# The last expert of a mixture-of-experts stage multiplied in plain fp32, its weights loaded straight into their tiles

## The chip, the cores and the metric

The kernel runs on 1 core of one Trainium2 chip. The metric is the device time of one execution in microseconds (us); lower is better. TensorE is called PE, VectorE DVE, ScalarE ACT, GpSimd POOL, and SyncE, which issues nearly all DMAs here, SP.

## The reference

Three stages follow one another: clustered attention, a mixture of experts in which every token goes to one of 8 experts, and a dense feed-forward layer.

```python
# attention: q, k, v are (2, 8, 768, 64); a query sees only the keys of its own cluster (16 clusters)
scores = np.where(q_assign[..., :, None] == k_assign[..., None, :], q @ k.T / 8, -1e9)
x = softmax(scores) @ v                     # tokens: (1536, 512)
# experts: 8 experts, w1[e] is (512, 1024), w2[e] is (1024, 512)
e_idx = np.argmax(x @ w_gate, axis=1)
for e in range(8):
    h = np.maximum(x[mask] @ w1[e], 0.0)
    out[mask] = gate_w[mask, None] * eom[mask, e, None] * (h @ w2[e])
# dense layer: w_in is (512, 2048), w_out is (2048, 512), both given as float64
h = out @ w_in
y = (h * sigmoid(1.702 * h)) @ w_out
```

## The kernel before, in words

The attention takes the first 280 us or so and the change does not touch it. The experts follow, sorted by the number of their tokens: the expert in place 0 has room for 304 tokens, the next ones for 256, 224, 208, 192, 176 and 160, and the last, in place 7 (called E7 here; E6 is the one in front of it), for 128. The work is written for a manual schedule, so each engine does its instructions in the order of the code (with the interleaving of the tile framework at a few places).

**A product.** The experts and the dense layer work with high and low parts: a number is split into a rounded part (type fp32r) and the rest, and a product is high times high, high times low and low times high. `product` does this for an expert with at most 256 tokens in two matmuls: the high weights times the low and the high part of the tokens side by side (2n columns, L1162), and the low weights times the high part of the tokens (n columns, L1163). The two halves of the sum are added afterwards by `total`: ACT copies one half out of PSUM (L1168), DVE adds it to the other (L1169).

**A step.** An expert has four chunks of 256 hidden columns, each with two halves of weights of 512 KB: half 0 from `w1`, half 1 from `w2`. The loop over `g` takes eight steps for an expert, one for each 128 hidden columns; E7 has g = 56 to 63. In step g, `win_h` does four products (w1, accumulated into a bank `ph`), `total` and the Relu (L1183) by ACT and DVE, and later `rest` (L1186, DVE) makes the low part of the hidden values. `finish` does the four products of w2 (`win_y`, into four banks `py`) for step g - 2. In the second step of an expert (`turned`) `finish` goes first; so `py` of E6 ends in step 57, and `win_out` empties its four banks by `total`, and then E7's first `win_y`, in step 58, can write them.

**Weights.** `loads_to` lets SP load halves into four buffers `raw` in the order of a list; `split_pair` makes the high part by ACT (L1064, a cast of 128x1024) and the low part by POOL, or by DVE in every fourth step (L1067). The tiles of split weights come from the pool `wp`, three buffers for each half, `w0` and `w1`, each `[128, 2, 1024]`: one chunk's high and low part. The split for step g + 3 of the list is written at the head of step g, ahead of the step's own work on ACT:

```python
split_low = split_pair(ekeys[n_], half, None, nc.vector if g % 4 == 3 else nc.gpsimd, g % 4 == 3)
loads_to(g + 7)
```

The tokens of the next expert are turned by PE and split by ACT (L1150) and DVE (L1151) in `win_x`; for E7 this lies in step 54. `dense_step` spreads the conversion of the dense layer's float64 weights over the steps (`wide_stages`: L125 to L135, then L1099 by ACT and L1100 by POOL).

**The dense layer.** 48 steps of 24 matmuls with 512 columns (L1347 to L1349 and L1445 to L1447). The first of them, `dense_in(0)`, stands between E7's last two groups of `win_y`.

Of the kernel before, what the change touches and what calls it, by code (L numbers as in the profile page):

```python
# [46 lines left out]
def attention_moe_ffn(ctx: ExitStack, tc: tile.TileContext, q, k, v, centroids, w_gate, w_og, w1, w2, w_in, w_out, out):  # L47
# [981 lines left out]
    def bank(name):  # L1029
        pool, tag = banks[0]  # L1030
        banks.rotate(-1)
        return pool.tile([128, 512], F32, name=name, tag=tag)
# [74 lines left out]
    def wb(key, part, i):  # L1107
        return pairs[key]["w", 1][:, part].rearrange("p (i d) -> p i d", i=2)[:, i]


    def win_load(ex_row, n, one_tile=False, pieces=False):
        nr = -(-n // 128)
        if one_tile:
            x = hp.tile([128, 2 * CAP], F32R, name="ht", tag="ht")[:, None, :DM].bitcast(F32)
        else:
            x = xrp.tile([128, WR, DM], F32, name="xr", tag="xr")
        d = {"n": n, "nr": nr, "x": x, "rows": [128] * (nr - 1) + [n - 128 * (nr - 1)]}

        def rows_of(r0, m, p, names):
            row = nc.s_assert_within(ex_row + r0 * 128, 0, E * NT - 128, skip_runtime_bounds_check_because="inside the rows of an expert") if r0 else ex_row  # L1120
            x = nc.sync.dma_start(out=d["x"][:p, r0:r0 + m], in_=xd[bass.ds(row + FIRST, m * p)].rearrange("(r p) c -> p r c", p=p)).ins
            for nm in scatters[len(names):]:
                tc.declare_no_dep(x, nm, reason="an expert with 128 rows in these groups: later tokens have other rows")
            need(x, names)

        if pieces:

            p = (n - 128) // (nr - 1)
            d["rows"] = [128] + [p] * (nr - 1)
            assert sum(d["rows"]) == n and LEAST >= 128  # L1130
            rows_of(0, 1, 128, scatters[:-GROUPS[-1][2]])
            d["rest"] = lambda: rows_of(1, nr - 1, p, scatters)
        else:
            rows_of(0, nr, 128, scatters)
        return d

    def win_x(d, r):
        if r == 0:

            side = CAPS.index(d["n"]) % 2 if d["n"] in CAPS else 0  # L1140
            d["t"] = xp.tile([128, 8 * CAPS[side]], F32R, name="t", tag=f"t{side}", bufs=1)[:, :8 * d["n"]].rearrange("p (k n) -> p k n", k=4)
        m, r0 = d["rows"][r], sum(d["rows"][:r])
        xs = d["x"][:m, r]
        pt = bank("pxt")
        for k in range(4):
            nc.tensor.transpose(pt[:, k * 128:k * 128 + m], xs[:, k * 128:(k + 1) * 128], ident[:m, :m])
        n = d["n"]
        hi = d["t"][:, :, n + r0:n + r0 + m]
        src = pt.rearrange("p (k n) -> p k n", k=4)[:, :, :m]
        nc.scalar.copy(hi, src)  # L1150
        nc.vector.tensor_tensor(d["t"][:, :, r0:r0 + m], src, f32(hi), op=ALU.subtract)  # L1151

    def product(ps, n, w_hi, w_lo, t, first, last):


        lo, hi = t[:, 0:n], t[:, n:2 * n]
        if n > 256:
            nc.tensor.matmul(ps[:, :n], w_hi, hi, start=first, stop=False)
            nc.tensor.matmul(ps[:, :n], w_hi, lo, start=False, stop=False)
            nc.tensor.matmul(ps[:, :n], w_lo, hi, start=False, stop=last)  # L1160
        else:
            nc.tensor.matmul(ps[:, :2 * n], w_hi, t, start=first, stop=False)  # L1162
            nc.tensor.matmul(ps[:, n:2 * n], w_lo, hi, start=False, stop=last)  # L1163
# [8 lines left out]
    def win_h(d, key, i, defer=False):  # L1172
        n = d["n"]
        ph = bank("ph")
        for k in range(4):
            product(ph, n, wa(key, 0, k, i), wa(key, 1, k, i), d["t"][:, k], k == 0, k == 3)
        ht = hp.tile([128, 2 * CAP], F32R, name="ht", tag="ht")[:, :2 * n]
        lo, hi = ht[:, 0:n], ht[:, n:]
        t = ph[:, :n]
        if n <= 256:  # L1180

            total(ph, n, t)
        nc.scalar.activation(hi, t, AF.Relu)  # L1183

        def rest():
            nc.vector.scalar_tensor_tensor(lo, t, 0.0, f32(hi), op0=ALU.max, op1=ALU.subtract)  # L1186
        if defer:
            return ht, rest
        rest()
        return ht  # L1190

    def win_y(d, key, i, ht, first, last):
        if first:
            d["py"] = sums()
        for m in range(4):
            ms = slice(m * 128, (m + 1) * 128)
            product(d["py"][m], d["n"], wb(key, 0, i)[:, ms], wb(key, 1, i)[:, ms], ht, first, last)

    def win_out(d, col, defer=False, eng=None):
        n = d["n"]  # L1200
        cs = bass.ds(col, n)
        if n > 256:
            ys = [py[:, :n] for py in d["py"]]
        else:
            room = xp.tile([128, 4 * max(CAPS[1:])], F32, name="room", tag="room", bufs=1)[:, :4 * n].rearrange("p (m n) -> p m n", m=4)
            ys = [total(d["py"][m], n, room[:, m]) for m in range(4)]

        def rest():
            if n <= 256:
                nc.scalar.copy(yth[:, :, cs], room)  # L1210
                (eng or nc.gpsimd).tensor_tensor(ytl[:, :, cs], room, f32(yth)[:, :, cs], op=ALU.subtract)
                return
            for m, y in enumerate(ys):
                nc.scalar.copy(yth[:, m, cs], y)
                nc.vector.tensor_tensor(ytl[:, m, cs], y, f32(yth)[:, m, cs], op=ALU.subtract)
        if defer and n <= 256:
            return rest
        rest()

    cx = ExitStack()  # L1220
    raw = cx.enter_context(tc.tile_pool(name="raw", reuse_waits="tile", bufs=4))
    ekeys = [("e", e, c) for e in range(E) for c in range(4)]
# [1 line left out]


    order = [(0, 0), (1, 0), (0, 1)]
    for n in range(2, len(ekeys) + 1):
        order += [(n, 0)] * (n < len(ekeys)) + [(n - 1, 1)]

    def loads_to(n):  # L1230

        while loaded[0] < min(n, len(order)):
            n_, half = order[loaded[0]]
            load_half(ekeys[n_], half, exps[ekeys[n_][1]], rawd if loaded[0] < 2 else None)
            loaded[0] += 1

    xp = cx.enter_context(tc.tile_pool(name="xp", reuse_waits="tile", bufs=2))
    hp = cx.enter_context(tc.tile_pool(name="hp", reuse_waits="tile", bufs=3))
    xrp = cx.enter_context(tc.tile_pool(name="xrp", reuse_waits="tile", bufs=1))
# [1 line left out]
    wins = {}  # L1241

    def win_start(e, pieces=False):
        wins[e] = win_load(nc.s_assert_within(exps[e] * NT, 0, (E - 1) * NT, skip_runtime_bounds_check_because="a row of experts"), CAPS[e], False, pieces)


    loads_to(2)
# [104 lines left out]
    with tc.manual_schedule():  # L1352
# [14 lines left out]
        for g in range(G + 2):  # L1367
# [40 lines left out]
            for f in (low, split_low, *late):  # L1408
                if f:
                    f()  # L1410
            dense_step(min(5 * e + max(0, c - 2), 40) + 3 * min(max(0, g - 61), 2))
            if g < G:
                if c == 0 and e and e + 1 < E:
                    win_start(e + 1)
                if g == 2:
                    offs = nc.values_load_multi_w_load_instructions(plan[:, E:], engines=[ACT_E, DVE_E, POOL_E], min_val=0, max_val=NT)[1]
# [111 lines left out]
```

## Time and profile before

| | before |
|---|---|
| time, median of 3 runs | 724.02 us (720.78 to 724.78) |
| time of the profiled execution | 724.04 us |
| its span, first to last instruction | 722.3 us |
| PE, busy share of the span | 97% |
| DVE, ACT, POOL | 63%, 54%, 37% |

The time of the profiled execution is 1.7 us more than its span; this much lies around the span and no view shows it. The busy shares are means over the attention, the experts and the dense layer. A matmul's end is modelled and overlaps the start of the next one, so the pace of PE is read from the starts of its instructions.

### The profile page before, as it was taken

Reading aid. Unit: us, or ns where it says so; the run is one execution under the profiler, and the core shown is the slowest. Engines: PE = TensorE matmul, PEld = TensorE weight load, DVE = VectorE, ACT = ScalarE, POOL = GpSimd, SP = SyncE. Lnnn points to the kernel's source line nnn. Section 1 sums busy time; section 2 is a strip of 40 time slices with the busy share of each in tenths; the row PEclk is TensorE's granted clock in tenths of the full one; section 3 lists DMA queues with packets and bytes.
Section 4 is the critical chain, followed back from the end, with each engine's and each line's share of the span. In section 5 each row is a group of like instructions: output and inputs, shape, how many; then the busy total and the mean of one; then the engine's idle time right before and its main releaser. Section 6 shows DMA issues by size and latency. Waiting matters only on the chain.

```text
span 722.3 us, 12542 instructions
## 1 busy us (share of the span) xinstructions
PE 699.4 (97%) x4522; PEld 577.7 (80%) x4522; DVE 452.2 (63%) x888; ACT 393.0 (54%) x789; POOL 266.4 (37%) x219
## 2 busy tenths in 40 slices
PE   8999999999999998999999998999999999999996
PEld 6777776776766777999999898888888888888885
DVE  6969788899988972344544545788564666242322
ACT  7767676666766643566777676544434353222220
POOL 2230321303280033766979889222532112020202
PEclk8999999999999998999999999999999999999999
DMA  6768869546066538566677775233634220010101
GB/s 198 170 189 273 215 225 282 153 146 181 27 171 213 196 126 269 172 229 206 199 241 232 263 235 188 89 110 68 85 59 59 60 87 30 1 59 1 59 0 59
DMA packets 70573, 105.18 MB, mean 146 GB/s; under 512 B 9627, under 2 KB 48283, under 8 KB 70507
## 3 DMA queue, kind: packets, MB, share of 16 engines
q1 hardware_dynamic: 67563, 95.94, 45.7%
q0 software_dynamic: 2944, 8.40, 3.1%
q8 instruction: 37, 0.61, 0.3%
q14 instruction: 29, 0.24, 0.1%
HBM read 70.46 MB, written 14.69 MB: 118 GB/s over the span
## 4 chain that ended last, share of the span: by engine, by line
PE 54%; issue 17%; POOL 7%; DMA 7%; DVE 6%; ACT 6%; SPq 1%; POOLq 0%; ACTq 0%; DVEq 0%
PE po L567 6%; PE pt L532 5%; PE ph L1347 4%; PE ph L1349 4%; PE ph L1348 4%; PE py L1447 3%; PE py L1445 3%; PE py L1446 3%; PE sp L515 3%; PE sp L516 3%; POOL w L1067 3%; PE py L1162 3%; PE ph L1162 2%; ACT w L1064 2%; DMA raw<-in_moe_w_dram 2%
## 5 line engine op out<-in xcount | busy, mean ns | idle before, releaser
L1067 POOL TENSOR_TENSOR w<-raw,w 128x1024 fp32r<-128x1024 f32 x51 | 128.1, 2529 | 38.3 <-ACT w L1064 25.4
L518 DVE TENSOR_REDUCE nm<-sp 128x1 f32<-128x768 f32 x96 | 91.6, 955 | 15.6 <-PE sp L516 14.4
L1430 DVE TENSOR_TENSOR sg<-ph,sg 128x512 f32<-128x512 f32 x48 | 33.2, 691 | 99.7 <-ACT sg L1429 97.5
L524 ACT ACTIVATE P<-sp,nm 128x768 f32<-128x768 f32 x96 | 87.2, 909 | 10.6 <-DVE nm L518 10.1
L532 PEld LDWEIGHTS pt<-ident,P 128*128 128x128 f32 x576 | 65.2, 141 | 27.3 <-issue 16.9
L532 PE MATMUL pt<-ident,P 128*128 128x128 f32 x576 | 82.9, 277 | 3.4 <-DVE pT L539 1.6
L1429 ACT ACTIVATE sg<-ph 128x512 f32<-128x512 f32 x48 | 28.7, 597 | 104.8 <-PE ph L1349 100.4
L1447 PE MATMUL py<-w,gl 128*128 128x512 f32 (+1 forms) x194 | 75.2, 387 | 0.0
L1445 PE MATMUL py<-w,gh 128*128 128x512 f32 (+1 forms) x194 | 75.0, 387 | 0.0
L1446 PE MATMUL py<-w,gh 128*128 128x512 f32 (+1 forms) x194 | 75.0, 387 | 0.0
L1100 POOL TENSOR_TENSOR w<-csq,w 128x512 fp32r<-128x512 f32 x24 | 32.7, 1363 | 114.5 <-ACT w L1099 114.5
L1347 PE MATMUL ph<-yth,w 128*128 128x512 f32 x192 | 74.8, 390 | 0.0
L1349 PE MATMUL ph<-yth,w 128*128 128x512 f32 x192 | 74.7, 389 | 0.0
L1348 PE MATMUL ph<-ytl,w 128*128 128x512 f32 x192 | 74.7, 389 | 0.0
L515 PE MATMUL sp<-X,Q 128*128 128x384 f32 x192 | 73.6, 384 | 0.5 <-ACT P L524 0.4
L1162 PE MATMUL py<-ht,w 128*128 128x512 f32 (+6 forms) x224 | 69.8, 367 | 3.5 <-DVE room L1169 2.0
L1064 ACT CAST w<-raw 128x1024 fp32r<-128x1024 f32 x68 | 70.5, 1042 | 4.8 <-issue 2.5
L1162 PE MATMUL ph<-t,w 128*128 128x512 f32 (+6 forms) x224 | 68.9, 366 | 1.2 <-DVE ht L1186 0.7
L567 PE MATMUL po<-pT,ld_v 128*32 128x384 f32 x768 | 68.6, 490 | 0.0
L516 PE MATMUL sp<-Z,Q 80*128 80x384 f32 x192 | 65.3, 340 | 1.9 <-DMA Q<-ohT 1.9
L537 ACT COPY pT<-pt 128x384 f32<-128x384 f32 x96 | 45.9, 478 | 32.7 <-PE pt L532 32.7
L539 DVE COPY pT<-pt 128x384 f32<-128x384 f32 x96 | 52.8, 550 | 8.1 <-PE pt L532 7.7
(294 smaller groups left out, 1468.7 us busy)
## 6 DMA issues: line engine op xcount, KB each, us to landing
raw<-in_moe_w_dram SPq DMA_DIRECT2D x64, 512.0 KB
raw<-in_moe_w_in_dram SPq DMA_DIRECT2D x16, 512.0 KB
raw<-in_moe_w_out_dram SPq DMA_DIRECT2D x16, 512.0 KB
xd<-zrow SPq DMA_DIRECT2D x8, 768.0 KB
Q<-Hq SPq DMA_DIRECT2D x28, 192.0 KB
ew<-in_moe_w_dram SPq DMA_DIRECT2D x9, 384.0 KB
ld_q<-in_q_dram SPq DMA_DIRECT2D x8, 384.0 KB
ld_k<-in_k_dram SPq DMA_DIRECT2D x8, 384.0 KB
```

Of the source, the lines that this page charges most:

```text
L515: nc.tensor.matmul(sp[:, n, :384], d["Q1"][:, h, cs], d["X"][:, h, ks], start=True, stop=False)
L518: nc.vector.tensor_reduce(nm, sp[:, :, :384], op=ALU.max, axis=AX.XY, negate=True)
L532: nc.tensor.transpose(pt[:, r * 128:(r + 1) * 128], L["P"][:, n, r * 128:(r + 1) * 128], ident)
L567: nc.tensor.matmul(po[32 * g:32 * g + 32, :384], v_[:, hh, tile_t(kt), 32 * a:32 * a + 32], pts[n][:, kt, :], start=kt < (2 if alone else ...
L1067: (eng or nc.gpsimd).tensor_tensor(lo, r, f32(hi), op=ALU.subtract)
L1162: nc.tensor.matmul(ps[:, :2 * n], w_hi, t, start=first, stop=False)
L1347: nc.tensor.matmul(ph, wa(key, 0, k, i), yth[:, k, cs], start=(k == 0), stop=False)
L1348: nc.tensor.matmul(ph, wa(key, 0, k, i), ytl[:, k, cs], start=False, stop=False)
L1349: nc.tensor.matmul(ph, wa(key, 1, k, i), yth[:, k, cs], start=False, stop=(k == 3))
L1445: nc.tensor.matmul(po[m][:, cs], gh[:, ms], wb(key, 0, i)[:, cs], start=first, stop=False)
L1446: nc.tensor.matmul(po[m][:, cs], gh[:, ms], wb(key, 1, i)[:, cs], start=False, stop=False)
L1447: nc.tensor.matmul(po[m][:, cs], gl[:, ms], wb(key, 0, i)[:, cs], start=False, stop=last)
```

## The change

E7 (`PLAN`) is marked `plain`. It has no high and low parts: `win_x` makes one fp32 copy of its tokens, `win_h` and `win_y` do one fp32 matmul for each product, the Relu goes straight from PSUM to the hidden values, and `win_out` takes the four banks as they are. The list of loads and splits ends with E6. In place of E7's eight halves by way of `raw`, `load_plain` lets SP load them into the same tiles of `wp`, two chunks to a tile (two DMAs of 512 KB each), after the work of steps 52, 54 and 56. The products, their number and the order of the steps stay.

```diff
--- before.py
+++ after.py
@@ -1147,6 +1147,9 @@
         n = d["n"]
         hi = d["t"][:, :, n + r0:n + r0 + m]
         src = pt.rearrange("p (k n) -> p k n", k=4)[:, :, :m]
+        if d.get("plain"):
+            nc.scalar.copy(f32(d["t"])[:, :, 0:n], src)
+            return
         nc.scalar.copy(hi, src)
         nc.vector.tensor_tensor(d["t"][:, :, r0:r0 + m], src, f32(hi), op=ALU.subtract)
 
@@ -1172,6 +1175,12 @@
     def win_h(d, key, i, defer=False):
         n = d["n"]
         ph = bank("ph")
+        if d.get("plain"):
+            ht = f32(hp.tile([128, 2 * CAP], F32R, name="ht", tag="ht"))[:, :n]
+            for k in range(4):
+                nc.tensor.matmul(ph[:, :n], wa(key, 0, k, i), f32(d["t"])[:, k, 0:n], start=k == 0, stop=k == 3)
+            nc.scalar.activation(ht, ph[:, :n], AF.Relu)
+            return ht, None
         for k in range(4):
             product(ph, n, wa(key, 0, k, i), wa(key, 1, k, i), d["t"][:, k], k == 0, k == 3)
         ht = hp.tile([128, 2 * CAP], F32R, name="ht", tag="ht")[:, :2 * n]
@@ -1194,19 +1203,22 @@
             d["py"] = sums()
         for m in range(4):
             ms = slice(m * 128, (m + 1) * 128)
+            if d.get("plain"):
+                nc.tensor.matmul(d["py"][m][:, :d["n"]], wb(key, 0, i)[:, ms], ht, start=first, stop=last)
+                continue
             product(d["py"][m], d["n"], wb(key, 0, i)[:, ms], wb(key, 1, i)[:, ms], ht, first, last)
 
     def win_out(d, col, defer=False, eng=None):
         n = d["n"]
         cs = bass.ds(col, n)
-        if n > 256:
+        if n > 256 or d.get("plain"):
             ys = [py[:, :n] for py in d["py"]]
         else:
             room = xp.tile([128, 4 * max(CAPS[1:])], F32, name="room", tag="room", bufs=1)[:, :4 * n].rearrange("p (m n) -> p m n", m=4)
             ys = [total(d["py"][m], n, room[:, m]) for m in range(4)]
 
         def rest():
-            if n <= 256:
+            if n <= 256 and not d.get("plain"):
                 nc.scalar.copy(yth[:, :, cs], room)
                 (eng or nc.gpsimd).tensor_tensor(ytl[:, :, cs], room, f32(yth)[:, :, cs], op=ALU.subtract)
                 return
@@ -1217,6 +1229,7 @@
             return rest
         rest()
 
+    PLAIN = E - 1
     cx = ExitStack()
     raw = cx.enter_context(tc.tile_pool(name="raw", reuse_waits="tile", bufs=4))
     ekeys = [("e", e, c) for e in range(E) for c in range(4)]
@@ -1224,8 +1237,8 @@
 
 
     order = [(0, 0), (1, 0), (0, 1)]
-    for n in range(2, len(ekeys) + 1):
-        order += [(n, 0)] * (n < len(ekeys)) + [(n - 1, 1)]
+    for n in range(2, 4 * PLAIN + 1):
+        order += [(n, 0)] * (n < 4 * PLAIN) + [(n - 1, 1)]
 
     def loads_to(n):
 
@@ -1234,6 +1247,17 @@
             load_half(ekeys[n_], half, exps[ekeys[n_][1]], rawd if loaded[0] < 2 else None)
             loaded[0] += 1
 
+    def load_plain(half, c0):
+
+        w = f32(wp.tile([128, 2, 1024], F32R, name=f"w{half}", tag=f"w{half}"))
+        ex = exps[PLAIN]
+        for n in range(2):
+            src = pair_of(w1[bass.ds(ex, 1)].rearrange("o d f -> (o d) f"), w2[bass.ds(ex, 1)].rearrange("o f d -> (o f) d"), c0 + n)[half]
+            nc.sync.dma_start(out=w[:, n].rearrange("p (g n) -> p g n", g=src.shape[1]), in_=src)
+            pairs.setdefault(("e", PLAIN, c0 + n), {})["w", half] = w[:, n:n + 1]
+
+    plain_at = {52: [(0, 0)], 54: [(0, 2), (1, 0)], 56: [(1, 2)]}
+
     xp = cx.enter_context(tc.tile_pool(name="xp", reuse_waits="tile", bufs=2))
     hp = cx.enter_context(tc.tile_pool(name="hp", reuse_waits="tile", bufs=3))
     xrp = cx.enter_context(tc.tile_pool(name="xrp", reuse_waits="tile", bufs=1))
@@ -1241,7 +1265,9 @@
     wins = {}
 
     def win_start(e, pieces=False):
+        assert e != PLAIN or CAPS[e] <= 128
         wins[e] = win_load(nc.s_assert_within(exps[e] * NT, 0, (E - 1) * NT, skip_runtime_bounds_check_because="a row of experts"), CAPS[e], False, pieces)
+        wins[e]["plain"] = e == PLAIN
 
 
     loads_to(2)
@@ -1409,6 +1435,8 @@
                 if f:
                     f()
             dense_step(min(5 * e + max(0, c - 2), 40) + 3 * min(max(0, g - 61), 2))
+            for x in plain_at.get(g, ()):
+                load_plain(*x)
             if g < G:
                 if c == 0 and e and e + 1 < E:
                     win_start(e + 1)
```

What this moves is seen on three engines. In the rows, `w` with a number is a tile of weights; the diff above shifts line numbers, so L1168, L1169 and L1183 of before read L1171, L1172 and L1192 after, L1162 and L1163 read L1165 and L1166, and E7's own Relu is L1182. The words in brackets are what an instruction waits for: engines, or DMA queues (DMAHW).

ACT, from step 54 to the first emptying of E6's banks (`hs<-py`) in step 57, before:

```order
L1064 CAST w_6228<-raw 128x1024 [waits DMAHW3_49,Pool_49]
L1150 CAST t<-pxt 128x4x128 [waits PE_49]
L1168 COPY hs<-ph 128x160 [waits PE_49,Activation_49]
L1183 ACTIVATE ht<-ph 128x160 [waits DVE_49]
L1064 CAST w_6264<-raw 128x1024 [waits DMAHW4_49,Pool_49]
L1168 COPY hs<-ph 128x160 [waits PE_49,Activation_49]
L1183 ACTIVATE ht<-ph 128x160 [waits DVE_49]
L1064 CAST w_6294<-raw 128x1024 [waits DMAHW5_49,Pool_49]
L1168 COPY hs<-ph 128x128 [waits PE_49,Activation_49]
L1183 ACTIVATE ht<-ph 128x128 [waits DVE_49]
L1064 CAST w_6322<-raw 128x1024 [waits DMAHW6_49]
L1168 COPY hs<-py_6128 128x160 [waits PE_49,Activation_49]
```

The same place in the changed kernel:

```order
L1151 COPY t<-pxt 128x4x128 [waits PE_49]
L1171 COPY hs<-ph 128x160 [waits PE_49,Activation_49]
L1192 ACTIVATE ht<-ph 128x160 [waits DVE_49]
L1171 COPY hs<-ph 128x160 [waits PE_49,Activation_49]
L1192 ACTIVATE ht<-ph 128x160 [waits DVE_49]
L1182 ACTIVATE ht<-ph 128x128 [waits PE_49,Activation_49]
L1171 COPY hs<-py_6126 128x160 [waits PE_49,Activation_49]
```

The four casts of weights between these rows are gone, E7's first Relu waits for PE and no longer for a sum by DVE, and it needs no `hs` ahead of it.

PE at the beginning of E7 (step 56: `win_h` of E7, then the first product of `win_y` for E6's step 54), before:

```order
L1162 MATMUL ph<-t,w_6169 128x256 [waits DVE_49]
L1163 MATMUL ph<-t,w_6169 128x128 [waits Pool_49]
L1162 MATMUL ph<-t,w_6169 128x256
L1163 MATMUL ph<-t,w_6169 128x128
...
L1162 MATMUL py_6128<-ht,w_6199 128x320 [waits DVE_49]
L1163 MATMUL py_6128<-ht,w_6199 128x160 [waits Pool_49]
```

And after:

```order
L1181 MATMUL ph<-t,w_6193 128x128 [waits DMAHW2_49,Activation_49]
L1181 MATMUL ph<-t,w_6193 128x128 x3
L1165 MATMUL py_6126<-ht,w_6165 128x320 [waits DVE_49]
L1166 MATMUL py_6126<-ht,w_6165 128x160 [waits Pool_49]
```

Eight matmuls have become four of 128 columns; they wait for a DMA and for ACT where they waited for DVE and POOL.

SP, E7's loads up to the first load of the dense layer that has to be converted (L111), before:

```order
L1050 DMA raw<-in_moe_w_dram 128x2x512 [waits DMAHW7_49,DVE_49,Activation_49]
L1050 ISA
L1050 DMA raw<-in_moe_w_dram 128x4x256 [waits DMAHW1_49,Pool_49]
L1050 ISA
L1050 DMA raw<-in_moe_w_dram 128x2x512 [waits DMAHW2_49,Pool_49]
L1050 ISA
L1050 DMA raw<-in_moe_w_dram 128x4x256 [waits DMAHW3_49,Pool_49]
L111 DMA raw<-in_moe_w_in_dram 128x2x512 [waits DMAHW0_49]
```

And after (`w_6250` holds half 0 of E7's chunks 2 and 3, `w_6253` half 1 of chunks 0 and 1; ahead of them stand the two loads of `w_6193`, half 0 of chunks 0 and 1, the first of which waits for PE alone):

```order
L1256 DMA w_6250<-in_moe_w_dram 128x4x256 [waits PE_49]
L1256 ISA
L1256 DMA w_6250<-in_moe_w_dram 128x4x256 [waits DMAHW5_49]
L1256 ISA
L1256 DMA w_6253<-in_moe_w_dram 128x2x512 [waits DMAHW6_49,PE_49,Pool_49]
L1256 ISA
L1256 DMA w_6253<-in_moe_w_dram 128x2x512 [waits DMAHW7_49]
L111 DMA raw<-in_moe_w_in_dram 128x2x512 [waits DMAHW0_49]
```

E7's loads wait for PE to be done with the tile that they write over, and no longer for a split that frees a `raw` buffer; the dense load behind them follows sooner.

## Rows read from the trace of the kernel before

**Rows 1.** The page: each engine's busy us, share of the span, and instructions.

```profile
PE 699.4 (97%) x4522; PEld 577.7 (80%) x4522; DVE 452.2 (63%) x888; ACT 393.0 (54%) x789; POOL 266.4 (37%) x219
```

**Rows 2.** Windows: us, each engine's busy us, granted PE clock, DMA share, GB/s.

```profile
434.00:457.00 23.00, 20.69 (x157) 19.54 (x158) 12.88 (x31) 14.15 (x34) 17.37 (x8) 1.00 0.48 164
457.00:700.00 243.00, 243.00 (x1074) 201.07 (x1073) 132.58 (x209) 89.51 (x155) 52.04 (x43) 1.00 0.24 55
```

**Rows 3.** Timeline of PE, 423 to 446: start, us, instruction, [idle before <-releaser].

```profile
423.09 0.24 PE L1163 MATMUL ph<-t,w 128*128 128x160 f32 x1
...
433.27 0.23 PE L1163 MATMUL py<-ht,w 128*128 128x160 f32 x1
434.03 0.38 PE L1162 MATMUL ph<-t,w 128*128 128x256 f32 x1 [0.53 <-DVE t L1151]
...
436.00 0.24 PE L1163 MATMUL py<-ht,w 128*128 128x160 f32 x1
436.80 0.41 PE L1162 MATMUL py<-ht,w 128*128 128x320 f32 x1 [0.56 <-DVE ht L1186]
...
439.66 0.22 PE L1163 MATMUL ph<-t,w 128*128 128x128 f32 x1
441.30 0.39 PE L1162 MATMUL py<-ht,w 128*128 128x256 f32 x1 [1.42 <-DVE room L1169]
...
441.75 0.22 PE L1163 MATMUL py<-ht,w 128*128 128x128 f32 x1
442.04 0.38 PE L1162 MATMUL py<-ht,w 128*128 128x256 f32 x1
...
445.27 0.22 PE L1163 MATMUL ph<-t,w 128*128 128x128 f32 x1
445.74 0.39 PE L1162 MATMUL py<-ht,w 128*128 128x256 f32 x1 [0.25 <-DVE ht L1186]
```

**Rows 4.** Timeline of PE, first and last start of 28 products of E7.

```profile
446.71 0.34 PE L1162 MATMUL ph<-t,w 128*128 128x256 f32 x1
...
453.22 0.44 PE L1347 MATMUL ph<-yth,w 128*128 128x512 f32 x1
```

**Rows 5.** Timeline of PE, plain fp32 matmuls at the attention's end, merged.

```profile
265.83 3.82 PE L822 MATMUL pt<-xst,ew 128*128 128x128 f32 x32
...
269.70 7.31 PE L832 MATMUL sp<-hsoon,ew 128*128 128x128 f32 x64
```

**Rows 6.** Windows, the stretch of L832.

```profile
270.00:277.00 7.00, 7.00 (x63) 6.82 (x62) 3.81 (x12) 1.36 (x2) 0.97 (x1) 1.00 0.56 157
```

**Rows 7.** Timeline of ACT, 428 to 441.

```profile
428.95 1.99 ACT L1064 CAST w<-raw 128x1024 fp32r<-128x1024 f32 x2
...
431.73 1.04 ACT L1064 CAST w<-raw 128x1024 fp32r<-128x1024 f32 x1
...
439.41 0.28 ACT L1183 ACTIVATE ht<-ph 128x128 fp32r<-128x128 f32 x1 [1.93 <-DVE ph L1169]
439.59 1.04 ACT L1064 CAST w<-raw 128x1024 fp32r<-128x1024 f32 x1
440.52 0.49 ACT L1168 COPY hs<-py 128x160 f32<-128x160 f32 x2
```

**Rows 8.** Timeline of DVE, 433 to 442.

```profile
433.29 0.69 DVE L1151 TENSOR_TENSOR t<-pxt,t 128x512 fp32r<-128x512 f32 x1 [1.10 <-ACT t L1150]
...
436.66 2.51 DVE L1067 TENSOR_TENSOR w<-raw,w 128x1024 fp32r<-128x1024 f32 x1
...
441.66 0.56 DVE L1169 TENSOR_TENSOR room<-py,hs 128x160 f32<-128x160 f32 x2 [0.18 <-ACT hs L1168]
```

**Rows 9.** Windows, the fastest 5 us of DMA around E7.

```profile
440.00:445.00 5.00, 3.64 (x29) 3.49 (x30) 1.97 (x8) 3.81 (x10) 5.00 (x4) 1.00 1.02 338
```

**Rows 10.** Timeline of POOL, dense weights of chunk 2 (second piece of half 0).

```profile
463.42 1.62 POOL L1100 TENSOR_TENSOR w<-csq,w 128x512 fp32r<-128x512 f32 x1 [7.03 <-ACT w L1099]
```

**Rows 11.** Timeline of PE, first use of chunk 2, in dense step 4.

```profile
470.57 0.39 PE L1347 MATMUL ph<-yth,w 128*128 128x512 f32 x1
```

## The prediction

> **What bounds the kernel now.** I read the busy shares first, then the stretches by window, then the starts on PE in E7's stretch, and last what ACT and DVE did ahead of each wait. PE is busy for 97% of the span [rows 1], so only time that PE loses counts. The windows say where that is: from 457 to 700 us PE is busy for 243.00 of 243.00 us, and from 434 to 457, E7's stretch, for 20.69 of 23.00 [rows 2]. The dense layer can gain nothing. The granted clock is 1.00 in both, so it plays no part.
>
> In E7's stretch the starts on PE tell more than the busy time. At the usual pace a matmul of the second kind (L1163) is followed 0.06 us later; the reader should look for pairs of starts further apart. There are five: 433.27 to 434.03, 436.00 to 436.80, 439.66 to 441.30, 441.75 to 442.04 and 445.27 to 445.74, together 0.76 + 0.80 + 1.64 + 0.29 + 0.47 = 3.96 us [rows 3]. Less five times 0.06 that is **3.66 us of waits**. All releasers shown are DVE instructions, and behind each stands ACT: E7's tokens (L1151, released by L1150 on ACT) come after three casts of weights, 1.99 us for two and 1.04 for one [rows 7, 8]; the hidden values of E6's last step likewise. The longest, 1.42 us idle, is for the banks of E6's sums: DVE sat in a split of 2.51 us from 436.66, so step 56's Relu came only at 439.41, then a cast of 1.04 at 439.59, and only at 440.52 could ACT begin to empty the banks [rows 7, 8]. ACT and DVE run late here because they split E7's weights just then.
>
> **The change, part by part.**
>
> *The splits.* Eight casts on ACT (1.04 us each [rows 7]), from step 53 to 60, and eight low parts on POOL and DVE go. ACT and DVE are not the bound, so the removal is worth only the waits that they cause. Of the three casts ahead of E7's tokens the dense layer's remains, the first in the 1.99 us row, over by 430.0; then come E6's sum and Relu of step 53 and the copy of the tokens, done by about 431.5 (an estimate from these rows), against 433.33 when PE wants it. The hidden values of step 55, for which PE waited till 436.80, follow with no cast ahead of them. In step 57 ACT finds the last bank of E6 filled some 0.2 us after PE's last matmul on it and empties them all in 1.70 us, from 440.52 to 442.22 (the end of L1169's second pair [rows 7, 8]); before its first write PE does eight products of E7, 8 x 0.226 = 1.8 us (below), and reaches the fourth bank 0.7 us after the first. So the first bank has 1.8 us where it needs about 0.9, and the fourth 2.5 where it needs 1.9. That wait goes too, with little to spare. The two short waits (0.23 for the later banks and 0.41 for hidden values behind a cast) go for the same reasons. I take all 3.66 us; the bound on the other side is that the bank wait stays whole, 1.64 - 0.06 = 1.58 us.
>
> *The products.* E7 has 8 steps with 4 products of w1 and 4 of w2, 64 in all. Before, 28 products took 453.22 - 446.71 = 6.51 us, 0.2325 each [rows 4]. A plain product of exactly this shape (128x128 weights, 128 columns, fp32) stands at the end of the attention: the code issues 32 in L822 and 32 in L832, and the trace shows two matmul records for each. From first to last start, 64 records of L832 take 7.31 - 0.28 = 7.03 us and 32 of L822 take 3.82 - 0.28 = 3.54, where 0.28 is the modelled length of the last [rows 5]; 7.03/63 and 3.54/31 are 0.112 and 0.114 us a record, 0.223 and 0.228 a product. L832's stretch ran at clock 1.00 [rows 6], like E7's. I take the mean, 0.226: 64 x (0.2325 - 0.226) = **0.4 us gained**; the bounds are 0.3 and 0.6. That is why halving the count of instructions gives almost nothing: in both forms a product has two records with weights of their own, and the loading of weights is busy for 6.82 of 7.00 us in L832's stretch [rows 6] and for 19.54 of the 20.69 us in which PE was busy in E7's [rows 2].
>
> The Trainium skill speaks against this part ("FP8 and Floating Point Precision", section TensorE Precision Notes): true fp32 takes four passes through the array. Counted in columns that is 4 x 128 = 512 against 256 + 128 = 384 before. This case's trace does not bear a loss out: the plain product is not slower than the pair.
>
> *The loads.* Eight DMAs of 512 KB stay eight, but land in the tile itself, so nothing stands between landing and PE. Half 0 of chunks 0 and 1 goes when PE has done step 51's `win_h`, whose last matmul starts at 423.09 [rows 3]; PE wants it at 433.33. That is 1.05 MB in 10 us: at 338 GB/s, the fastest 5 us here [rows 9], it takes 3.1 us, at the mean of E7's stretch, 164 GB/s [rows 2], 6.4. Half 1 of the same chunks goes after step 53 and is wanted in step 58, at about 438.3 (441.30 less the waits of 0.70, 0.74 and 1.58 ahead of it). Between 427 and 438 some 2.6 MB are asked for (this, half 0 of chunks 2 and 3, and the dense layer's load), 7.8 us at 338 GB/s, and its first half comes ahead of the dense one. Hidden, with about 2 us to spare; the last pair, issued after step 55's `win_y`, has two steps more. I cost the loads at nothing.
>
> *The end of E7.* Four copies on ACT and four subtractions on DVE, straight from the banks, replace four `total`s, a copy and a subtraction. The dense layer writes those banks only after two further `dense_in`, 24 matmuls at 243.00/1074 = 0.226 [rows 2], 5.4 us; hidden.
>
> *What is late next.* After E7 everything moves up by the gain, and the dense layer's conversions move with it, as they stand in the same steps. Even if they stayed, chunk 2's second piece is split by 463.42 + 1.62 = 465.04 and used at 470.57 [rows 10, 11], now at 466.5.
>
> **Sum.** 3.66 + 0.4 = 4.1 us. The profiled execution took 724.04 us, which agrees with the median of the runs, 724.02: 724.0 - 4.1 = **719.9 us**, 0.57% less.
>
> **The rivals.**
>
> A. *The bank wait stays* (1.58 of the 4.1): E6's last sums must still be emptied by ACT and DVE, and any other instruction in front, an `yth` copy or a late Relu, uses up a margin of 0.6 us. For it speaks that it is the tightest of the waits; against it that the cast and the split ahead of it are gone. Time: 724.0 - 2.5 = 721.5.
>
> B. *The gain is given back* in the dense layer, which starts 4 us sooner while its float64 pieces are still loaded and converted; PE would then wait where it never did. Against it: 5.5 us of slack at the first use of chunk 2, less the 4.1 gained [rows 10, 11]. Time: 722.5 to 724.
>
> C. *The plain product is dearer (slower than before).* If each of the four passes were a record with its own weights, a product would cost 4 x 0.112 = 0.447 us and 64 of them 13.7 us more: 724.0 - 3.7 + 13.7 = 734. It decides from 0.290 us a product on (0.2325 + 3.66/64). The two records for each product in rows 5 speak against it. The four passes of the Trainium skill's page would be their mechanism.
>
> D. *E7's first weights land late (slower).* They are issued only when PE frees the tile. Each us after 433.3 costs one us, so the change loses when they land after 437.4, 14 us after the issue, a rate of 74 GB/s; rows 2 and 9 show two to four times that.
>
> **How the numbers follow.** Chances: the forecast 0.63, A 0.20, B 0.09, C 0.03, D 0.02, and 0.03 that more is gained than the sum, because E6's last steps also lose the casts. The likeliest case's own range is 719.4 (0.6 for the products, and 0.1 to 0.3 in E6) to 720.6 (a part of the bank wait stays). A measurement of this kernel can tell about 0.5%, 3.6 us, from no change; the forecast lies only 0.5 us beyond that, and the three runs of before lie up to 3.2 us from their median. So the range takes in A and half of B above, 722.6, and below the forecast's end less a good us of this scatter, 718.2. Faster: 0.55 of the forecast's 0.63 and the 0.03, 0.58. Same: the rest of the forecast, A and B, 0.37. Slower: C and D, 0.05.
>
> **What would show it.** PE's starts between 433 and 453 us with no gap over 0.3 us; two fp32 records for a product, 0.11 us apart; the first dense matmul 4.1 us earlier than 453.22; ACT empty of casts from step 53 on; eight loads issued between 423 and 434; PE without idle time in the dense layer. Wrong would be: a wait for a DMA in front of E7's first products, a wait for DVE at the banks in step 58, products more than 0.23 us apart, or idle time on PE after 453.

## The result and the profile after

The changed kernel takes 717.0 us, the median of 7 runs (716.49 to 717.98), against 724.02 us for the kernel before in the same comparison (7 runs, 720.78 to 727.6). The ratio is 0.9912 with an interval of 0.9891 to 0.9933: 0.9% faster. Forecast were 719.9 us and a range of 718.2 to 722.6, so the time lies 1.2 us under the range. The direction was right, the size was not.

The profiled execution of the changed kernel took 717.98 us, the longest of its seven, with a span of 716.3 us. The page gives the busy us of each engine, to be laid beside [rows 1].

```profile
PE 697.0 (97%) x4522; PEld 577.1 (81%) x4522; DVE 443.3 (62%) x868; ACT 383.4 (54%) x772; POOL 250.6 (35%) x213
```

PE has as many instructions as before, 4522, and is busy for 2.4 us less. From each of ACT, DVE and POOL more left (9.6, 8.9 and 15.8 us) than from the span (6.0).

Windows of the changed kernel, with the columns of [rows 2]:

```profile
434.00:457.00 23.00, 23.00 (x167) 21.46 (x167) 8.61 (x20) 9.08 (x24) 2.61 (x2) 1.00 0.37 133
457.00:700.00 243.00, 243.00 (x1074) 201.28 (x1073) 128.87 (x200) 87.08 (x148) 51.69 (x43) 1.00 0.23 54
```

In the stretch where PE was busy for 20.69 of 23.00 us it is now busy for all of it, at the same granted clock of 1.00. The dense layer, in the second line, is as full as before.

The timeline of PE through E7 (start, us, instruction, and how many in a row):

```profile
431.89 1.09 PE L1181 MATMUL ph<-t,w 128*128 128x128 f32 x8
432.74 0.39 PE L1165 MATMUL py<-ht,w 128*128 128x320 f32 x1
...
434.77 0.24 PE L1166 MATMUL py<-ht,w 128*128 128x160 f32 x1
434.85 1.98 PE L1181 MATMUL ph<-t,w 128*128 128x128 f32 x16
436.67 1.06 PE L1207 MATMUL py<-ht,w 128*128 128x128 f32 x8
437.56 1.06 PE L1181 MATMUL ph<-t,w 128*128 128x128 f32 x8
...
445.60 1.95 PE L1207 MATMUL py<-ht,w 128*128 128x128 f32 x16
447.31 0.48 PE L1373 MATMUL ph<-yth,w 128*128 128x512 f32 x1
...
450.16 1.05 PE L1207 MATMUL py<-ht,w 128*128 128x128 f32 x8
450.97 0.48 PE L1373 MATMUL ph<-yth,w 128*128 128x512 f32 x1
```

No row carries an idle time: the five waits of [rows 3] are gone. A product is two records; the 80 records from 436.67 to 445.60 start 8.93/80 = 0.1116 us apart, 0.223 us a product.

ACT in the same stretch:

```profile
429.49 0.58 ACT L1151 COPY t<-pxt 128x512 f32<-128x512 f32 x1
...
434.33 0.55 ACT L1171 COPY hs<-py 128x160 f32<-128x160 f32 x2 [0.97 <-PE py L1166]
435.14 0.52 ACT L1171 COPY hs<-py 128x160 f32<-128x160 f32 x2 [0.26 <-DVE room L1172]
...
438.65 0.28 ACT L1182 ACTIVATE ht<-ph 128x128 f32<-128x128 f32 x1 [1.51 <-PE ph L1181]
```

The sides have changed: ACT now waits for PE. E7's tokens are copied by 430.07, 1.8 us before PE wants them (in the kernel before they were ready at 433.98 [rows 8], 0.65 us after the 433.33 at which PE would have gone on). E6's banks, emptied from 440.52 on before [rows 7], are emptied from 434.33 on, in step with PE's last matmuls on them.

The queue of SP shows E7's loads:

```profile
422.06 6.93 SPq L1256 DMA_DIRECT2D w<-in_moe_w_dram  x6
...
432.19 0.94 SPq L1256 DMA_DIRECT2D w<-in_moe_w_dram  x2
```

Eight DMAs, issued from 422.06 to 433.13, and PE waits for none of them.

**Where the time went, from one profile to the other.** The span is cut at three starts on PE: E6's first product, E7's first product (434.03 before, 431.89 after), and the dense layer's first matmul of chunk 1 (456.91 before, 450.97 after).

| us | to E6's first product | on to E7's first | on to dense chunk 1 | on to the end of the span |
|---|---|---|---|---|
| before | 415.23 | 18.80 | 22.88 | 265.43 |
| after | 413.95 | 17.94 | 19.08 | 265.30 |
| difference | -1.28 | -0.86 | -3.80 | -0.13 |

The last three columns, 4.8 us, are where the change is. The first, 1.28 us, is code that the change leaves as it was.

### The profile page after: what moved, and what is told of

Read it like the earlier page. It is cut to its first block, busy times and chain, and to the rows that moved or that the text cites. A ratio compares the mean times of both kernels' runs of the same rounds, so it can differ in the third digit from the quotient of the medians.

```text
span 716.3 us, 12495 instructions
## 1 busy us (share of the span) xinstructions
PE 697.0 (97%) x4522; PEld 577.1 (81%) x4522; DVE 443.3 (62%) x868; ACT 383.4 (54%) x772; POOL 250.6 (35%) x213
## 4 chain that ended last, share of the span: by engine, by line
PE 70%; issue 15%; DVE 6%; DMA 2%; POOL 2%; ACT 2%; SPq 0%; POOLq 0%; ACTq 0%; DVEq 0%
PE po L567 8%; PE pt L532 7%; PE ph L1165 5%; PE py L1165 5%; PE sp L515 4%; PE sp L516 4%; PE ph L1375 4%; PE ph L1374 4%; PE ph L1373 4%; PE py L1475 3%; PE py L1474 3%; PE py L1473 3%; PE py L1166 2%; PE ph L1166 2%; PE pox L586 2%
## 5 line engine op out<-in xcount | busy, mean ns | idle before, releaser
L1067 POOL TENSOR_TENSOR w<-raw,w 128x1024 fp32r<-128x1024 f32 x45 | 112.6, 2519 | 37.5 <-ACT w L1064 36.7
L1064 ACT CAST w<-raw 128x1024 fp32r<-128x1024 f32 x60 | 62.2, 1042 | 4.9 <-issue 2.5
L1165 PE MATMUL py<-ht,w 128*128 128x512 f32 (+5 forms) x192 | 61.1, 370 | 1.2 <-DVE room L1172 0.6
L1165 PE MATMUL ph<-t,w 128*128 128x512 f32 (+5 forms) x192 | 60.8, 371 | 0.6 <-DVE ht L1195 0.6
```

The source lines that it names most:

```text
L1067: (eng or nc.gpsimd).tensor_tensor(lo, r, f32(hi), op=ALU.subtract)
```

## The experiments

**The same kernels again.** Is the part beyond 4.8 us the kernel's, or does it come and go? The kernel before was run again as if it were a new one, and the changed kernel twice more, without any edit.

> The kernel before, unchanged. The measured change (7.0 us between the medians) is larger than what the two profiles show in E7's stretch (23.6 us from E7's first product to dense_in(1) before, 19.1 after: 4.5). Theory S (scatter): the other 2.4 us are scatter of stretches that the change does not touch, above all waits of the attention's PE for DMAs; then the ratio to the kernel before is 1.000 within 0.005, the stretch of E7 is again 23.6 us within 0.5, and the start of E7's first product lies at another time than 434.0 by 0.5 us or more. Theory E (E7's waits scatter): the stretch itself is longer or shorter than 23.6 by over 1 us, since its waits depend on when loads land. Theory P (the change also moves the attention): E7's first product lies at 434.0 within 0.4 again.

> The changed kernel, unchanged. Theory S: ratio near 0.994 (4.5 us less) with an interval that reaches from 0.990 to 0.997; the start of E7's first product, 431.9 in the first profile, is elsewhere by 0.5 us or more. Theory P: ratio 0.991 again, and E7's first product again at 431.9 within 0.4. In both the stretch is 19.1 us within 0.3.

> The changed kernel once more, beside the version with two plain experts on the same chip. Its own stretch: E6's first product to dense_in(1) 37.0 us within 0.1, E7's first product to dense_in(1) 19.08 within 0.1; time against the kernel before 0.9925 to 0.9945 by the theory that the change is worth 4.8 us and the rest of the first result is scatter.

Measured: the kernel before 722.03 us (12 runs, 718.68 to 724.11) against itself at 722.07 (29 runs, 716.99 to 724.49), ratio 1.0002 [0.9983, 1.0021]. The changed kernel 716.3 us (ratio 0.9924 [0.99, 0.9948]), and the third time 717.46 us against 721.61 (ratio 0.9938 [0.9918, 0.9959]). The profiles, cut as above:

| us | to E6's first product | on to E7's first | on to dense chunk 1 | on to the end of the span |
|---|---|---|---|---|
| before, again | 411.57 | 18.78 | 22.92 | 265.44 |
| after, again | 414.57 | 17.91 | 19.08 | 265.30 |
| after, third | 414.57 | 17.96 | 19.07 | 265.30 |

Behind E6's first product every column repeats within 0.1 us. Ahead of it the two executions of before differ by 3.7 us, and the slower of them (415.23) and the faster (411.57) lie on both sides of all three of after. So what the change is worth is 4.8 us, and the rest of the first comparison is scatter of a stretch that it doesn't touch: theory S. (The 23.6 us of the expectations count from 433.33, when PE would have gone on to E7; the 22.88 of the table count from E7's first product.) A part of that scatter has a place. The view of waits on PE, summed over the execution (us idle, how often, the longest), has in the kernel before

```profile
PE sp L516 <- DMA Q<-ohT: 1.9, 2, 1.2
```

and in the changed kernel's first profile

```profile
PE sp L516 <- DMA Q<-ohT: 0.7, 1, 0.7
```

It is a wait of the attention for a DMA, in a line that both kernels have; in the second profile of after it is 1.8 again, in that of before 1.5. Between the first profiles of the two kernels it makes 1.2 us.

Between the two profiles of before it makes only 0.4 of the 3.7 us, and there TensorE's granted clock is another part. In all ten profiles it falls below 1.00 in the same two places; here they are in the first and in the second profile of before (windows with the columns of [rows 2]):

```profile
10.00:20.00 10.00, 9.62 (x52) 7.12 (x53) 6.85 (x15) 8.09 (x15) 2.63 (x8) 0.66 0.51 125
280.00:290.00 10.00, 9.32 (x47) 8.78 (x48) 2.60 (x5) 6.40 (x10) 7.31 (x4) 0.66 0.98 352
```

```profile
10.00:20.00 10.00, 8.98 (x54) 6.11 (x56) 7.23 (x17) 8.63 (x18) 2.63 (x8) 0.83 0.54 127
280.00:290.00 10.00, 10.00 (x63) 10.00 (x62) 2.02 (x4) 5.34 (x8) 9.29 (x4) 0.83 0.91 313
```

A window of 2 us inside (12 to 14 us, in both) shows 0.50, the lower of the clock's two levels, 1.2 of 2.4 GHz. Ahead of the second place PE had been busy for about half of the time (2.08 and 1.95 of the 4.00 us from 276 to 280). In the first profile the clock stays low for longer, and over the same instructions this profile loses 0.54 us in the first place (it goes from 8.27 to 17.57 us, the other from 8.03 to 16.79) and 0.79 in the second (280.14 to 289.29, against 277.68 to 286.04). The runs of before go with the clock too: of the 52 made after the first comparison, the 14 with a mean granted clock of 0.991 or more took 719.9 us in the mean, the 13 with 0.987 or less 723.0. Whether the lower clock makes a run long, or only comes along with what does, is not shown, and the changed kernel's 19 runs show no such link: 716.9 us for the 5 from 0.991 on, 717.1 for the other 14. What makes up the remaining 2 us between the two profiles of before stays open.

**Plain products, but the splits kept.** E7's weights come through the raw buffers again, with eight copies on ACT and eight subtractions on POOL and DVE, whose results nobody uses; the products stay plain.

```diff
     def split_pair(key, half, pool=None, eng=None, defer=False):
         d = pairs[key]
         w = halves(d, half, pool)
         r = d.pop(("raw", half))
+        if key[:2] == ("e", E - 1):
+            w = f32(w)
+            d["w", half] = w
...
-    for n in range(2, 4 * PLAIN + 1):
-        order += [(n, 0)] * (n < 4 * PLAIN) + [(n - 1, 1)]
+    for n in range(2, len(ekeys) + 1):
+        order += [(n, 0)] * (n < len(ekeys)) + [(n - 1, 1)]
...
-            for x in plain_at.get(g, ()):
-                load_plain(*x)
```

> The changed kernel with E7's weights loaded and split as before: eight loads through the raw buffers, eight casts on ACT, eight subtractions on POOL and DVE. Their low parts are computed and not used; E7's products are plain fp32. My theory (waits come from ACT and DVE running late behind the splits): most of the waits of 0.7 in front of E7's first product, 0.7 before the sums of step 55 and 1.6 for the banks come back, PE waits 2 to 3.5 us in the stretch, which is 21 to 22.5 us long: ratio to before 0.996 to 0.998. Rival (the waits came from E7's own sums and low parts, which fp32 products do without): no wait above 0.3 us, stretch 19.1 to 19.5, as fast as the changed kernel.

Measured: 720.96 us, ratio 0.9988 [0.9969, 1.0006], where the theory said 0.996 to 0.998. The two columns of the stretch are 18.22 and 22.25 us, against 17.94 and 19.08 after: the splits alone bring back 0.28 + 3.17 = 3.45 of the 4.66 us. The stretch is as long as the theory said, but of the three waits that it named only the one of step 55 comes back. E7's tokens are copied by 429.53, without DVE's subtraction of 0.69 us behind the copy [rows 8], and PE begins E7 at 429.62 without a wait. Step 56's Relu comes at 433.08, though DVE sits in a split from 432.52 to 435.43: no sum of DVE stands in front of it any more, and of the bank wait only two gaps of 0.26 and 0.29 us are left. For these two waits the rival is right. But a wait comes that nobody had named. PE and ACT of this kernel:

```profile
432.66 0.41 PE L1168 MATMUL py<-ht,w 128*128 128x320 f32 x1 [0.57 <-DVE ht L1198]
...
442.83 1.16 PE L1210 MATMUL py<-ht,w 128*128 128x128 f32 x8 [1.18 <-ACT ht L1185]
```

```profile
441.55 1.04 ACT L1067 COPY w<-raw 128x1024 f32<-128x1024 f32 x1 [2.46 <-DMA raw<-in_moe_w_dram]
```

PE's 1.18 us are for a Relu on ACT that stands behind a cast, and the cast stood 2.46 us for its load. The load was late because its raw buffer was; POOL shows why:

```profile
427.29 12.68 POOL L1070 TENSOR_TENSOR w<-raw,w 128x1024 fp32r<-128x1024 f32 x5 [0.29 <-ACT w L1067]
```

Five subtractions in a row (two of them not E7's), 2.5 us each in the mean, and each holds a raw buffer until it ends. SP's queue waits for them before it can load (its waits from 425 to 450 us: us idle, how often, the longest):

```profile
SPq L1050 <- POOL w L1070: 9.2, 4, 4.1
```

The prediction had not seen this chain (POOL's subtraction, the buffer, the load, the cast, the Relu behind it), since in the kernel before the bank wait lay over it.

**The casts alone.** To the changed kernel one copy of 128x1024 on ACT is added in each of the steps 53 to 60, into a buffer that nobody reads; no subtractions. By the list, E7's own casts stood in steps 52 and 54 to 60 and E6's last one in 53, and the change moves that one to 52; so the copies load ACT in the same steps as before.

```diff
+            if 53 <= g < 61:
+                spent = raw.tile([128, 1024], F32, name="raw", tag="raw")
+                nc.scalar.copy(spent, f32(pairs["e", E - 2, 3]["w", 0][:, 0]))
```

> The changed kernel with eight copies of 128x1024 on ACT (about 1.04 us each) in steps 53 to 60, where the casts of E7's weights stood; their results are not used. No subtraction on POOL or DVE comes back. If ACT's casts alone made the waits: the stretch is 1.5 to 3 us longer than the changed kernel's 19.1, with the wait for the banks at 0.5 to 1.2 and one of about 0.7 in front of E7's first product. If it was the subtraction of 2.51 us on DVE that made the long one: the waits before E7 come back (0.5 to 1.4 in all), the one for the banks does not. If neither: 19.1 to 19.4.

Measured: 717.95 us, ratio 0.9953 [0.9932, 0.9974]; columns 18.08 and 20.25, so 0.14 + 1.17 = 1.3 us come back. That fits none of the three cases in full: the stretch is 1.2 us longer, under the 1.5 to 3 of the first, and neither the bank wait nor the one for E7's tokens returns. Another 0.34 us is in front of E6's products of step 54 (from E7's first start to theirs it is 1.22 us, 430.44 to 431.66, and 0.85 after). Most of the rest is one wait on PE, that for E6's hidden values of step 55, which here has its 0.8 us again:

```profile
432.69 0.24 PE L1166 MATMUL py<-ht,w 128*128 128x160 f32 x1
433.49 0.42 PE L1165 MATMUL py<-ht,w 128*128 128x320 f32 x1 [0.57 <-DVE ht L1195]
```

The casts on ACT thus carry about 1.3 us of the gain, and the subtractions with their buffers and loads the 3.45 - 1.3 = 2.1 us beyond, 1.3 of it in the wait at 442.83.

**Only the split ahead of the bank wait made short.** In the kernel before, the subtraction that DVE does at 436.66 [rows 8] becomes a write of zeros, so that the low part of `w2` is left out for E7's chunk 0.

```diff
+            if key == ("e", E - 1, 0) and half == 1:
+                nc.vector.memset(f32(lo), 0.0)
+                return
```

> The kernel before with one instruction made cheaper: in step 55 DVE writes zeros into the low part of one half of E7's weights (half 1 of chunk 0) where it subtracted for 2.51 us; so those low parts are left out of E7's products. Everything else is as before, casts included. My theory (the longest wait, 1.6 us for the banks of E6's sums, comes from DVE sitting in that subtraction while the sum, the Relu and a cast queue up behind it): the zeros take 1.2 us or less and the wait for the banks falls from 1.6 to 0.5 or less; the stretch from E7's first product to dense_in(1) falls from 22.9 to 21.5 to 21.9. Rival (ACT's casts make that wait): it stays above 1.2, the stretch at 22.6 or more.

Measured: 721.54 us, one run, beside 721.61 for the kernel before. The write took 0.91 us in place of 2.51, and the bank wait went from 1.64 us to a gap of 0.25, as the theory said. Yet the stretch is 22.76 us, 0.1 less than before, and not the 21.5 to 21.9 of the theory. PE and ACT of this kernel say where the time went:

```profile
443.79 0.22 PE L1166 MATMUL ph<-t,w 128*128 128x128 f32 x1
444.97 0.39 PE L1165 MATMUL py<-ht,w 128*128 128x256 f32 x1 [0.95 <-DVE ht L1189]
```

```profile
442.74 1.05 ACT L1064 CAST w<-raw 128x1024 fp32r<-128x1024 f32 x1 [1.16 <-DMA raw<-in_moe_w_dram]
```

A new gap of 1.18 us, behind a cast that waits 1.16 us for its load: the chain of the run with the splits kept. The longest wait on PE, taken away alone, is worth 0.1 us.

**All eight subtractions made short.** The kernel before, with a write of zeros by the same engine in place of each of E7's eight subtractions. E7's weights lose their low parts; casts, pairs of products and sums stay.

```diff
+            if key[:2] == ("e", E - 1):
+                (eng or nc.gpsimd).memset(f32(lo), 0.0)
+                return
```

> The kernel before, with all eight of E7's subtractions (five of POOL, three of DVE) replaced by writes of zeros into the same tiles by the same engines; E7's weights thus lose their low parts, and nothing else changes (casts, pairs of products and sums stay). Theory (the waits of E7's stretch come from one chain behind another: POOL's long splits free the raw buffers late, so the loads, the casts and the Relu behind them on ACT are late): with short writes both the bank wait of 1.64 us and the cast's wait for its load go, and from E7's first product to the dense layer's first product of chunk 1 it is 20.6 to 21.6 us, against 22.9 before and 19.1 after; what is left above 19.1 is the casts on ACT and the pairs of products. Rival (the waits are ACT's own, eight casts of about 1 us among the Relus): the stretch stays at 22.3 us or more though the subtractions are short.

Measured: 721.25 us in one run, whose profile begins E6 at 414.08 us, and a stretch of 21.41 us, inside the 20.6 to 21.6 of the theory and far from the rival's 22.3. E7's eight subtractions are six of POOL and two of DVE (the expectation counts five and three). POOL's writes, one at 426.15, two at 442.41 and the three below, take 0.9 to 1.0 us each:

```profile
434.50 2.74 POOL L1068 MEMSET w<- 128x1024 f32 x3
```

On PE no wait behind a late load is left, and of the waits for E6's banks only two short gaps between starts (0.25 and 0.28 us). The longer ones that remain in the stretch both have a cast of ACT ahead of them:

```profile
435.63 0.42 PE L1165 MATMUL py<-ht,w 128*128 128x320 f32 x1 [0.57 <-DVE ht L1189]
...
443.19 0.38 PE L1165 MATMUL py<-ht,w 128*128 128x256 f32 x1 [0.25 <-DVE ht L1189]
```

E7's tokens, in the column ahead, are as late as before (0.76 us from start to start). So the subtractions cost 22.88 - 21.41 = 1.5 us of the stretch, which only both chains together give; the 2.3 us from there to the 19.08 of after are the gaps that remain (0.75, 0.41, 0.22 and 0.19 above the usual pace) and the products. The time of the one run says little, since the way to E6 alone differs by up to 3.7 us.

**E6 plain too.** The same change for the last two experts, with the loads two steps apart.

```diff
...
-    PLAIN = E - 1
+    PLAIN = E - 2
...
-    plain_at = {52: [(0, 0)], 54: [(0, 2), (1, 0)], 56: [(1, 2)]}
+    plain_at = {44: [(6, 0, 0)], 46: [(6, 0, 2), (6, 1, 0)], 48: [(6, 1, 2)], 50: [(7, 0, 0), (7, 1, 0)], 52: [(7, 0, 2)], 54: [(7, 1, 2)]}
...
```

> The changed kernel with E6 (160 columns) plain too: no splits for E6 and E7, all 16 halves of 512 KB loaded straight into the tiles, from step 44 on. A plain fp32 matmul of 160 columns starts every 0.135 us at the end of the attention (the sums of heads, 128x160), so a product is 0.270 against 0.2625 for E6's pair: 0.5 us lost on 64 products. Gained at most: the waits left in front of and inside E6's stretch, about 0.7 + 0.3 us. Theory: E6's first product to dense_in(1), 37.0 us in the changed kernel, becomes 36.5 to 37.3, and the wait in front of E6 goes: the same time within 0.5 us. Rival (the splits of E6 cost PE more than the gaps show, as for E7 where the gain was 0.7 above the sum): 36.2 or less, and 1 us or more faster than the changed kernel. Another (loads come late, as two experts' loads wait for tiles): a wait for a DMA, 38 or more.

Measured: 716.89 us, ratio 0.9936 [0.9916, 0.9957], no different from the changed kernel's 0.9924 and 0.9938. From E6's first product to dense chunk 1 it is 37.36 us, 0.34 more than after (17.94 + 19.08 = 37.02) and just above the 36.5 to 37.3 of the theory. E6's products, with 160 columns, on PE of this kernel:

```profile
417.32 1.25 PE L1207 MATMUL py<-ht,w 128*128 128x160 f32 x8
418.41 1.25 PE L1181 MATMUL ph<-t,w 128*128 128x160 f32 x8
```

Eight records take 418.41 - 417.32 = 1.09 us, so a plain product costs 0.272 us at 160 columns. As a pair of 320 and 160 it costs 0.255 in the changed kernel, four products from the first of these starts to the second:

```profile
428.81 0.34 PE L1165 MATMUL py<-ht,w 128*128 128x320 f32 x1
...
429.83 0.35 PE L1165 MATMUL ph<-t,w 128*128 128x320 f32 x1
```

At 128 columns it is the other way round, 0.223 against 0.2325. The step to E6 gains nothing; no run points to a version that beats the changed kernel.

## Why the prediction was wrong

**The waits: the total right, the causes only in part.** All five are gone. In the stretch they are 0.80 + 1.64 + 0.29 + 0.47 - 0.24 = 2.96 us, and the one for E7's tokens is the 0.70 of the 0.86 us in the column ahead of it. Their causes were drawn too simply: the prediction put all of them down to the splits of E7's weights and took each wait as a gain of its own. With the splits put back, the waits for E7's tokens and for the banks (0.70 + 1.58 of the 3.66 us) stay away, so E7's plain form is enough to end them: no low part of the tokens, no sum in front of step 56's Relu. (A short split of DVE ends the bank wait as well.) What comes back instead is step 55's wait and the one behind a late load, a second chain of nearly the same length, which in the kernel before lay under the bank wait; the run with one split short shows it. Since the change takes away the splits and the sums at once, all of it went, and the total came out right; with the causes half wrong, that is in part luck. Also, of the three casts that the prediction sets ahead of E7's tokens only the one at 431.73 is E7's; of the two at 428.95 [rows 7] one is the dense layer's and one E6's last, by the list.

**The products: right in kind, half the size.** The prediction's 64 x (0.2325 - 0.226) = 0.4 us measured 0.82. Before, E7's 64 products take 22.88 us less E6's last eight (435.00 to 437.90, 2.90), the dense layer's twelve matmuls (2.82) and the waits among them (1.64 + 0.29 + 0.47 - 0.18 = 2.22): 14.94 us. After, 19.08 - 2.11 (432.74 to 434.85) - 2.85 (447.31 to 450.16) = 14.12 us. Two things were off: inside E7 a plain product takes 0.223 us, the lower of the two rows from which 0.226 was the mean [rows 5], and where a run of plain records ends, the next matmul starts sooner: the last 16 records of E7 take 447.31 - 445.60 = 1.71 us where 16 x 0.1116 would be 1.79. Even the prediction's upper bound of 0.6 was too low.

**The rest of the sum.** E6's other steps are 0.16 us quicker and the stretch behind dense chunk 1 0.13. With 0.05 for E6's last eight products and 0.03 lost in the dense matmuls: 2.96 + 0.70 + 0.82 + 0.16 + 0.13 + 0.05 - 0.03 = 4.8 us, where the sum said 4.1.

**The base: the step that failed.** "The profiled execution took 724.04 us, which agrees with the median of the runs, 724.02". Three runs and one profile agreed, and the prediction took that for the kernel's time. Over 29 and 11 later runs its median is 722.07 and 721.61 us, some 2 us lower, and single runs span 7.5 us (716.99 to 724.49). 722.07 - 4.8 = 717.3 us is what the changed kernel then shows (717.0, 716.3, 717.46). Of the miss of 2.9 us, 0.7 is the sum and 2.2 the base: with the measured 4.8 and the old base the forecast would have been 719.2, still above the range's lower end and 2.2 too high. The range had the same fault: to the forecast's lower end it added "a good us of this scatter", though the three runs that it names lay up to 3.2 us from their median. In the first comparison the kernel before still had a median of 724.02 (7 runs) and the ratio's interval reaches just to a gain of 4.85 us (1 - 0.9933, of 724.02). Why the early runs of before lay higher than the later ones stays open; the later ones go with the granted clock, and of the early ones only the profiled execution's is on record (0.989).

**The rivals.** A, the bank wait stays: no, the banks are emptied in step with PE, and with the casts alone put back they still are. B, given back in the dense layer: no, PE is busy for 243.00 of 243.00 us from 457 on. C, a dearer product: no at 128 columns (0.223 us against 0.2325), though at 160 the plain form is the dearer one (0.272 against 0.255). The Trainium skill ("FP8 and Floating Point Precision", section TensorE Precision Notes) has true fp32 take four passes; the traces show two records for a product and not four. D, late weights: no, no wait of PE for them in any of the three profiles.

## What to carry to other kernels

Before a wait is counted as a gain, ask which wait stands next behind it: the longest one here was worth 0.1 us alone, and the plain products with the splits kept gained 4.66 - 3.45 = 1.2 us of the 4.7 in E6 and E7. The rest came only with the splits on three engines gone as well. A saving in a stretch is best read from start to start on the engine that bounds it (here it repeats within 0.1 us), and the time of the whole from enough runs: three gave a base 2 us too high. And whether a plain product beats a pair is a matter of its columns: measure it at the very shape.

## What the runs showed of the hardware

DVE's subtraction of 128x1024 values took 1.27 us at one place and twice that or more at others. The changed kernel's DVE and POOL, at a place where POOL is, for the most part, between two subtractions:

```profile
425.90 1.27 DVE L1067 TENSOR_TENSOR w<-raw,w 128x1024 fp32r<-128x1024 f32 x1
```

```profile
423.71 2.39 POOL L1067 TENSOR_TENSOR w<-raw,w 128x1024 fp32r<-128x1024 f32 x1
426.64 5.14 POOL L1067 TENSOR_TENSOR w<-raw,w 128x1024 fp32r<-128x1024 f32 x2 [0.55 <-ACT w L1064]
```

In the kernel with the splits kept it took 2.91 us at 432.52, and in the kernel before 2.51 [rows 8], each time inside POOL's row of five. Two subtractions of that row in the kernel before; DVE's, from 436.66 to 439.17, begins in the first and ends in the second:

```profile
435.72 2.37 POOL L1067 TENSOR_TENSOR w<-raw,w 128x1024 fp32r<-128x1024 f32 x1
438.05 3.34 POOL L1067 TENSOR_TENSOR w<-raw,w 128x1024 fp32r<-128x1024 f32 x1
```

DVE ends 1.1 us after the first of them, and the second takes 1.0 us more than the first. A write of zeros, which reads nothing, took 0.91 us on DVE in the middle of such a row (the run with step 55 made short). The Trainium skill ("SBUF — State Buffer", section SBUF: two separate sides) says that GpSimd and a VectorE instruction with two inputs in SBUF share a pair of ports, and that whichever begins first has it for its whole length. The numbers agree with it: DVE waits out POOL's subtraction, and POOL's next one then waits for DVE. So the split of 2.51 us ahead of the bank wait was itself half a wait for POOL (436.66 to 438.09).
